# Recurrent attention into an ELU feed-forward layer: decay weights by summed logarithms on TensorE and ScalarE instead of scans on VectorE

## The chip, the cores and the metric

The kernel runs on one core of a Trainium2 chip. The metric is the device time of one execution in microseconds (us); smaller is better. The core has a matrix engine (TensorE, PE in the rows; its weight loads are PEld), a vector engine (VectorE, DVE), an activation engine (ScalarE, ACT), a general engine (GpSimd, POOL) and a queue engine (SyncE, SP) that issues all the DMA transfers here. Each engine runs its own instructions in program order and waits on semaphores for the others.

## What is computed

The reference is a recurrence over 768 steps for 4 batches of 8 heads of width 40, and then a feed-forward layer on all 3072 tokens (320 to 2048 to 320):

```python
for t in range(S):
    m_new = np.maximum(f_gate[:, :, t] + m, i_gate[:, :, t])
    f_stab = np.exp(f_gate[:, :, t] + m - m_new)
    i_stab = np.exp(i_gate[:, :, t] - m_new)
    m = m_new
    C = f_stab * C + i_stab * outer(vt, kt)
    n = f_stab * n + i_stab * kt
    y[:, :, t] = o * (C @ qt) / np.maximum(np.abs(n . qt), 1.0)
h = x @ w_in
g = np.where(h > 0.0, h, np.exp(np.minimum(h, 0.0)) - 1.0)
out = g @ w_out
```

## The kernel before

The recurrence is done in chunks of 128 steps. There are 6 chunks (`c`) and 4 batches (`b`), so 24 token blocks, n = 4c + b, called t0 to t23; each holds 128 tokens of all 8 heads. For one token block TensorE makes the products of keys and queries (`products`, L572), the weight of source step s at target step t is the product of the decays between them, the weighted products are multiplied with the values (`outputs`, L648; from chunk 1 on also the state of the earlier chunks, L640), and the state C of the batch is brought up to date (`update`, L661; the keys are first scaled by the last weights, `wl`). A result goes through a division, a gate and a transpose (L719) and is split in a high and a low part, `xh` and `xl`.

**The weights of a block.** For each half of the heads (4 heads, a tile of 128 x 512) VectorE runs a scan (`decays`, L612) along the targets: state = decay times state plus an identity entry. The decays must stand on all 128 partitions. For the first two chunks TensorE spreads them: `spread` (L598) multiplies a selecting matrix with the decays, cut in three bf16 parts (`parts`, L469 and L471), into a PSUM tile of the pool `h`, which has two buffers and serves the feed-forward layer's first results and the weight conversions too. From chunk 2 on a DMA does it. The input gates' factors are turned by TensorE (L484) and multiplied into the values (`va`, L580).

**The feed-forward layer** works on groups of two or three token blocks (2, 3, 3, ...) and 16 groups of 128 hidden units (f). One step is a first layer into `h` (eight matmuls, L772, 256 or 384 columns), an ELU on ScalarE and VectorE (L780, L783, L785), a split in two parts (L788, L790), and a second layer (L799). The first units of work are t0-t1 with f 0 to 7, t2-t4 with f 0 to 7, t5-t7 with f 0 to 7, and then t0-t1 again with f 8 to 15. The feed-forward weights come in as 64-bit words and are converted on the chip, 18 conversions c0, c1, ...; each is two ScalarE operations (L327, L332), three on VectorE (L336, L341, L346), one on GpSimd (L351), a rounding on ScalarE (L357) and the difference on VectorE (L361) or, for four of them, on TensorE (L369, L370).

**What sets the order.** All operations are recorded with the engines that may run them and a cost for each, and a list planner (`Plan.run`) then puts them out: by rank, then by the longest tail, on the engine that would end first, as far as the pools have room (`room`). `FIRST` gives the ranks of the first token blocks (t) and conversions (c). So an edit to costs, pools or operations moves instructions on every engine.

Of the kernel before, what the change touches and what calls it, by code (L numbers as in the profile page):

```python
# [11 lines left out]
F32 = mybir.dt.float32  # L12
# [8 lines left out]
P = 128  # L21
# [162 lines left out]
def tile_mlstm_then_elu_ffn(  # L184
# [27 lines left out]
    SPREAD_BY_PE = 2  # L212
# [6 lines left out]
    FIRST = "t0c0c4t1c5c6c1c2t2c8c3c7c9"  # L219
# [7 lines left out]
        wide=3, narrow=2, gates=2, rest=1, qk=3, bb=3, vko=3, w=3, va=2, wl=2, dec=2, den=2, xf=2,  # L227
# [27 lines left out]
    for name in room:  # L255
        if name not in ("ps_a", "h", "acc", "qk", "bb", "rest"):
            pool(name)
    pools["rest"] = ctx.enter_context(tc.tile_pool(name="rest", bufs=1))
# [127 lines left out]
    fgs = const.tile([3 * BH, SPREAD_BY_PE * L], BF16, name="fgs")  # L386
# [18 lines left out]
    def setup():  # L405
# [11 lines left out]
        op({"port": 1, "POOL": 0.8, "DVE": 0.4}, select, (("ident", 0),), (("sel", 0),))  # L417
        op({"POOL": 0.7, "DVE": 0.6},
# [12 lines left out]
    def gate_chunk(c):  # L431
# [18 lines left out]
        def log_decay(e):  # L450
            nc.vector.tensor_add(f(), f(), m()[:, 0:L])
            nc.vector.tensor_sub(f(), f(), m()[:, 1:])

        op({"port": 1, "DVE": 0.54}, log_decay, (KM,), (KF,))
        op({"port": 1, "POOL": 0.4, "DVE": 0.27}, lambda e: eng[e].tensor_sub(i(), i(), m()[:, 1:]), (KM,), (KI,))
        op({"ACT": 0.3}, lambda e: nc.scalar.activation(f(), f(), AF.Exp), (), (KF,))
# [7 lines left out]
        def parts(e):  # L464
            starts(e)
            rest = [f()] + [pools["rest"].tile([BH, L], F32, name=f"rest{j}") for j in range(2)]
            for j in range(3):
                part = fgs[j * BH : (j + 1) * BH, c * L : (c + 1) * L]
                nc.vector.tensor_copy(part, rest[j])  # L469
                if j < 2:  # L470
                    nc.vector.tensor_sub(rest[j + 1], rest[j], part)  # L471

        if c < SPREAD_BY_PE:
            op({"port": 1, "DVE": 1.5}, parts, (KF,), (FI, KF, ("fgs", c)))
        else:
            op({"port": 1, "DVE": 0.2}, starts, (KF,), (FI, KF))
            op({"SP": 0.06}, lambda e: nc.sync.dma_start(f_d[c], f()), (KF,), (("f_d", c),),
               nbytes=BH * L * 4)
# [9 lines left out]
        if c > 0:  # L488

            op({"port": 1, "DVE": 0.42},  # L490
# [39 lines left out]
    def attention(n):  # L530
# [15 lines left out]
        def va():  # L546
            return T("va", n, P, H, E)
# [381 lines left out]
```

## Time and profile before

| | |
|---|---|
| time of the three runs | 488.93, 490.2, 491.02 us; median 490.2 |
| span of the profiled execution, first to last instruction | 485.9 us |
| TensorE busy | 457.6 us, 94% of the span |
| VectorE busy | 366.3 us, 75% |
| ScalarE busy | 299.1 us, 62% |
| GpSimd busy | 85.5 us, 18% |

The profile gives no time of its own for the profiled execution beside its span; the median of the runs is 4.3 us over the span. The busy shares are means over a beginning, in which blocks are prepared and weights converted, and a long rest. Whether an engine is a limit is read by stretch. The granted clock of TensorE is one of two levels, 2.4 GHz (1.00) and 1.2 GHz (0.50).

### The profile page before, as it was taken

The page shows a single profiled execution, that of the slowest core. Times are in us where ns is not written, and L with a number is a line of the kernel's source. Part 1 is how long each engine was busy: PE and PEld are TensorE (multiplying, and loading weights), DVE is VectorE, ACT ScalarE, POOL GpSimd, SP SyncE. Part 2 cuts the span into 40 slices and gives each one's busy share as a digit, 9 for nine tenths or more (in the row PEclk, how much of TensorE's full clock was granted, in tenths as well). Part 3 has the DMA queues.
Part 4 walks back from the last instruction along what each step waited for, and adds up shares of the span by engine and source line. Part 5 has one row for each costly group of instructions (what it writes and reads, how often), then busy time and mean ns, then how long its engine had stood idle before and what let it go on. Part 6 is the DMA issues. An engine that isn't in the chain of part 4 may idle for free.

```text
span 485.9 us, 13150 instructions
## 1 busy us (share of the span) xinstructions
PE 457.6 (94%) x5342; PEld 429.9 (88%) x5342; DVE 366.3 (75%) x733; ACT 299.1 (62%) x753; POOL 85.5 (18%) x99
## 2 busy tenths in 40 slices
PE   2877889999999999999999999999999999999997
PEld 2554778899989999998999999999999999999996
DVE  8998799998988998959686578848778635446543
ACT  3778866668877555655456456665546654655764
POOL 3542263342230142212010002000001000000000
PEclk9779899999999999999999999999999999999999
DMA  7576454323325264424332233413324200100000
GB/s 254 184 222 210 137 167 138 112 99 125 109 82 155 77 191 138 136 72 125 102 109 69 76 89 107 125 40 113 112 89 137 70 1 1 42 1 4 28 0 28
DMA packets 39004, 49.56 MB, mean 102 GB/s; under 512 B 3072, under 2 KB 31648, under 8 KB 38944
## 3 DMA queue, kind: packets, MB, share of 16 engines
q1 hardware_dynamic: 38944, 48.72, 32.2%
q8 instruction: 42, 0.69, 0.6%
q14 instruction: 18, 0.15, 0.1%
HBM read 43.32 MB, written 5.39 MB: 100 GB/s over the span
## 4 chain that ended last, share of the span: by engine, by line
PE 80%; DVE 12%; ACT 3%; DMA 2%; issue 1%; SPq 1%; POOL 0%; DVEq 0%; ACTq 0%
PE h L772 35%; PE acc L799 32%; PE ps_a L572 5%; PE ps_a L648 2%; PE ps_a L640 2%; PE ps_a L719 1%; PE ps_a L661 1%; DMA qk<-in_qk 1%; DVE vko L698 1%; DVE C L672 1%; DVE w L612 1%; DVE e L785 1%; DVE gl L790 1%; DVE w L361 1%; ACT e L783 1%
## 5 line engine op out<-in xcount | busy, mean ns | idle before, releaser
L772 PE MATMUL h<-xh,w 128*128 128x384 f32 (+1 forms) x720 | 182.1, 326 | 3.8 <-DVE w L612 2.8
L799 PE MATMUL acc<-w,gh 128*128 128x320 f32 x768 | 173.6, 313 | 1.3 <-DVE w L361 1.2
L772 PEld LDWEIGHTS h<-xh,w 128*128 128x128 f32 x720 | 126.7, 190 | 7.1 <-DVE w L612 3.6
L799 PEld LDWEIGHTS acc<-w,gh 128*128 128x128 f32 x768 | 128.1, 188 | 3.3 <-DVE w L361 1.4
L799 PE MATMUL acc<-w,gl 128*128 128x320 f32 x384 | 119.2, 310 | 1.3 <-DVE gl L790 1.3
L785 DVE SCALAR_TENSOR_TENSOR e<-e,h 128x384 f32<-128x384 f32 (+1 forms) x144 | 72.8, 505 | 59.4 <-ACT e L783 58.6
L772 PE MATMUL h<-xl,w 128*128 128x384 f32 (+1 forms) x432 | 113.0, 320 | 2.0 <-DVE w L361 2.0
L780 ACT ACTIVATE e<-h 128x384 f32<-128x384 f32 (+1 forms) x144 | 65.4, 454 | 71.3 <-PE h L772 65.0
L790 DVE TENSOR_TENSOR gl<-e,gh 128x384 fp32r<-128x384 f32 (+1 forms) x126 | 68.7, 546 | 31.6 <-ACT gh L788 30.9
L788 ACT CAST gh<-e 128x384 fp32r<-128x384 f32 (+1 forms) x144 | 68.0, 472 | 31.1 <-DVE e L785 30.3
L772 PEld LDWEIGHTS h<-xl,w 128*128 128x128 f32 x432 | 77.7, 191 | 2.2 <-DVE w L361 2.2
L799 PEld LDWEIGHTS acc<-w,gl 128*128 128x128 f32 x384 | 72.2, 188 | 2.1 <-DVE gl L790 1.9
L783 ACT ACTIVATE e<-e 128x384 f32<-128x384 f32 (+1 forms) x144 | 70.5, 490 | 3.6
L612 DVE TENSOR_TENSOR_SCAN w<-w,ident 128x512 f32<-128x512 f32 x32 | 39.2, 1231 | 5.2 <-DMA w<-f_d 5.2
L351 POOL TENSOR_TENSOR narrow<-narrow,wide 128x512 int32<-128x512 int32 (+1 forms) x18 | 26.8, 1489 | 51.7 <-DVE narrow L346 20.2
L587 ACT ACTIVATE vko<-vko 128x320 f32<-128x320 f32 x72 | 33.4, 466 | 1.4 <-DMA vko<-in_vko 0.6
L626 DVE TENSOR_TENSOR w<-ps_a,w 128x512 f32<-128x512 f32 x48 | 31.4, 680 | 1.8 <-PE ps_a L572 1.8
L572 PE MATMUL ps_a<-qk 40*128 40x128 f32 x384 | 30.4, 298 | 0.0
L572 PEld LDWEIGHTS ps_a<-qk 40*128 40x128 f32 x384 | 25.6, 199 | 5.0 <-issue 3.5
L790 POOL TENSOR_TENSOR gl<-e,gh 128x384 fp32r<-128x384 f32 (+1 forms) x18 | 17.9, 994 | 58.2 <-ACT gh L788 49.3
L580 POOL TENSOR_TENSOR va<-vko,iT 128x320 f32<-128x320 f32 x16 | 12.8, 804 | 69.9 <-PE ps_a L661 28.2
L648 PE MATMUL ps_a<-va,w 128*32 128x41 f32 x1536 | 20.7, 207 | 3.5 <-DVE w L626 3.4
(96 smaller groups left out, 417.9 us busy)
## 6 DMA issues: line engine op xcount, KB each, us to landing
vko<-in_vko SPq DMA_DIRECT2D x24, 480.0 KB
w<-f_d SPq DMA_DIRECT2D x32, 256.0 KB
qk<-in_qk SPq DMA_DIRECT2D x48, 160.0 KB
wide<-in_w_out SPq DMA_DIRECT2D x8, 640.0 KB
wide<-in_w_in SPq DMA_DIRECT2D x8, 512.0 KB
out<-os SPq DMA_DIRECT2D x24, 160.0 KB
bb<-b_d SPq DMA_DIRECT2D x40, 80.0 KB
sum<-os SPq DMA_DIRECT2D x8, 160.0 KB
```

Source lines behind the costliest of these rows:

```text
L572: nc.tensor.matmul(ps(two, P, HH, L)[:, j, :], kt[rows, j, :], qt[rows, j, :], start=True, stop=True,)
L587: lambda e, fn=fn, kw=kw: nc.scalar.activation(v3()[2], v3()[2], fn, **kw), (), (KS,))
L612: nc.vector.tensor_tensor_scan(a, f, ident4.rearrange("p h t -> p (h t)"), 0.0, op0=ALU.mult, op1=ALU.add)
L626: lambda e, half=half: nc.vector.tensor_mul(w(half), ps(half, P, HH, L), w(half)),
L648: nc.tensor.matmul(y[r, h, :], w()[:, i, r], va()[:, h, :], start=not opened, stop=(i == H - 1), skip_group_check=True,)
L772: nc.tensor.matmul(h(), a[g][:, fs], m, start=(i == 0), stop=(i == len(prods) - 1))
L780: op(act(N), lambda e, h=h, ff=ff: nc.scalar.activation(ff("e"), h(), AF.Relu, scale=-1.0), (KHP,), (KE,))
L783: lambda e, ff=ff: nc.scalar.activation(ff("e"), ff("e"), AF.Exp, scale=-1.0), (), (KE,))
L785: lambda e, h=h, ff=ff: nc.vector.scalar_tensor_tensor(out=ff("e"), in0=ff("e"), scalar=-1.0, in1=h(), op0=ALU.add, op1=ALU.max),
L788: op(act(N), lambda e, ff=ff: nc.scalar.copy(ff("gh", F32R), ff("e")), (KE,), (KG,))
L790: lambda e, ff=ff: eng[e].tensor_sub(ff("gl", F32R), ff("e"), ff("gh", F32R).bitcast(F32)),
L799: nc.tensor.matmul(acc(a), x[:, sl], bw[g][:, j, :], start=(f == f0 and i == 0), stop=(f == f1 - 1 and i == 2),)
```

## The change

Five things change in the program.

First, for chunks 0 and 1 (`LOGS = 2`) the weights are no longer scanned. The logarithms of the decays are summed along the chunk on 32 partitions (one short scan), the input gate's logarithm minus that sum is put beside it, and both are cut in three bf16 parts (`lcs`, two rows of 128 instead of one). TensorE then makes the logarithm of every weight in an `h` tile from a mask (0, or minus 2 to the 100th where the source is later than the target), the source's term and the target's term, and one exponential on ScalarE writes the weights. The input gate is within them, so in these chunks no turned factor and no multiplication of the values is needed.

Second, the values come with a column of room for the ones from the DMA, and `va` is a view of that tile.

Third, the state update is part of `outputs`. It writes to the same PSUM tile as the outputs, in pieces of 32 and 8 columns, so `outputs` also waits for the scaled keys, and a token block takes one tile less of `ps_a`.

Fourth, `FIRST` is another list. Fifth, with the new operations the planner's order is another one on every engine.

```diff
-    SPREAD_BY_PE = 2
+    LOGS = 2
-    FIRST = "t0c0c4t1c5c6c1c2t2c8c3c7c9"
+    FIRST = "t0c3t1c4c0c1t2c2c5c6c9c10c11"
...
-        wide=3, narrow=2, gates=2, rest=1, qk=3, bb=3, vko=3, w=3, va=2, wl=2, dec=2, den=2, xf=2,
+        wide=3, narrow=2, gates=2, qk=3, bb=3, vko=3, w=3, wl=2, dec=2, den=2, xf=2,
...
+        if c < LOGS:
+            def sums_of_logs(e):
+                nc.vector.memset(lc()[:, 0, 0:1], 0.0)
+                nc.vector.tensor_tensor_scan(
+                    lc()[:, 0, 1:], f()[:, 1:], first[:, 1:], 0.0, op0=ALU.add, op1=ALU.min)
...
+            op({"port": 1, "DVE": 0.27}, lambda e: nc.vector.tensor_sub(lc()[:, 1], i(), lc()[:, 0]), (KI,), (KLC,))
...
+            def parts(e):
+                for j in range(3):
+                    part = lcs[j * BH : (j + 1) * BH, c]
+                    nc.vector.tensor_copy(part, lc())
+                    if j < 2:
+                        nc.vector.tensor_sub(lc(), lc(), part)
...
-                for j in range(HH):
-                    r = b * H + heads[half * HH + j]
+                mine = [b * H + h for h in heads[half * HH : (half + 1) * HH]]
+                nc.tensor.matmul(
+                    logs(), ident_b, mask.unsqueeze(1).to_broadcast([P, HH, L]),
+                    start=True, stop=False, skip_group_check=True,
+                )
+                nc.tensor.matmul(
+                    logs(), lcs[:, c, 1],
+                    sel[:, mine[0] : mine[-1] + 1 : 2].unsqueeze(2).to_broadcast([3 * BH, HH, L]),
+                    start=False, stop=False, skip_group_check=True,
+                )
+                for j, r in enumerate(mine):
                     nc.tensor.matmul(
-                        T("h", ("w", n, half), P, HH, L)[:, j, :],
-                        sel[:, r : r + 1].to_broadcast([3 * BH, P]),
-                        fgs[:, c * L : (c + 1) * L], start=True, stop=True,
+                        logs()[:, j, :], sel[:, r : r + 1].to_broadcast([3 * BH, P]), lcs[:, c, 0],
+                        start=False, stop=(j == HH - 1), skip_group_check=True,
                     )
...
-            if c < SPREAD_BY_PE:
-                op({"DVE": 1.23}, decays, (KP, ("ident4", 0)), (KW,))
+            if c < LOGS:
+                op({"PE": 0.8}, spread,
+                   (("sel", 0), ("lcs", c), ("mask", 0), ("ident_b", 0), ("w", n, "room")), (KP,))
+                op(act(HH * L),
+                   lambda e, half=half, logs=logs: nc.scalar.activation(w(half), logs(), AF.Exp), (KP,), (KW,))
...
+            if c < NC - 1:
+                for j in range(HH):
+                    for two, rows in enumerate(ROWS):
+                        for a, z in ((0, 32), (32, D)):
+                            nc.tensor.matmul(
+                                state()[rows.start + a : rows.start + z, j, :],
+                                v3()[1][:, 2 * j + two, a:z], va()[:, 2 * j + two, :],
+                                start=True, stop=True, skip_group_check=True,
+                            )
```

The order of the instructions moves with it. The first place is VectorE's work on the gates of chunk 0, up to what the first spread waits for. Before, the decays are cut in parts (`fgs`) and the first long scan follows:

```order
L452 TENSOR_TENSOR gatesf_158<-gatesf_158,gatesm_188 32x128
L455 TENSOR_TENSOR gatesi_166<-gatesi_166,gatesm_188 32x128
L461 COPY first_130<-gatesf_158 32x1
L462 MEMSET gatesf_158 32x1
L469 CAST fgs_131<-gatesf_158 32x128
L471 TENSOR_TENSOR rest0_204<-gatesf_158,fgs_131 32x128
L469 CAST fgs_131<-rest0_204 32x128
L471 TENSOR_TENSOR rest1_205<-rest0_204,fgs_131 32x128
L469 CAST fgs_131<-rest1_205 32x128
L580 TENSOR_TENSOR va_216<-vko_168,iT_133 128x8x40
L612 SCALAR_TENSOR_TENSOR w_229<-h_218,ident4_134 128x512
```

Now the logarithms are bounded (L467), summed (L480), subtracted (L484) and cut (L494 and L496, of which two more casts and one more difference follow):

```order
L465 TENSOR_TENSOR gatesf_154<-gatesf_154,gatesm_190 32x128
L467 TENSOR_SCALAR gatesf_154<-gatesf_154 32x128
L479 MEMSET gateslc_199 32x1
L480 SCALAR_TENSOR_TENSOR gateslc_199<-gatesf_154,first_124 32x127
L470 TENSOR_TENSOR gatesi_162<-gatesi_162,gatesm_190 32x128
L484 TENSOR_TENSOR gateslc_199<-gatesi_162,gateslc_199 32x128
L494 CAST lcs_125<-gateslc_199 32x256
L496 TENSOR_TENSOR gateslc_199<-gateslc_199,lcs_125 32x256
```

The chain to the first spread has more steps, and the steps of the cutting have twice the columns; the two exponentials that stood in it on ScalarE are gone.

The second place is TensorE at the end of block t0's weights. Before, a head's spread is one weight load and one matmul of 128 columns, and outputs and update follow as 32 and 8 instructions:

```order
L598 LDWEIGHTS sel_132
L598 MATMUL h_256<-fgs_131,sel_132 128x128
L648 MATMUL ps_a_269<-va_216,w_229 32x41 x32
L661 MATMUL ps_a_306<-va_216,vko_168 40x41 x8
L598 LDWEIGHTS sel_132
```

Now the half begins with two matmuls of 512 columns (mask and source term), and the update stands in pieces of 32 and 8 columns that alternate, 16 in all, in the outputs' own tile:

```order
L633 LDWEIGHTS ident_b_127
L633 MATMUL h_259<-mask_126,ident_b_127 128x512
L637 LDWEIGHTS lcs_125
L637 MATMUL h_259<-sel_128,lcs_125 128x512
L643 LDWEIGHTS sel_128
L643 MATMUL h_259<-lcs_125,sel_128 128x128
...
L695 MATMUL ps_a_272<-vko_164,w_243 32x41 x32
L705 MATMUL ps_a_272<-vko_164 32x41
L705 MATMUL ps_a_272<-vko_164 8x41
```

The third place is ScalarE after the fourth first-layer step of the feed-forward layer (`e` and `gh` are that layer's, `narrow` and `wide` a conversion's). Before, the layer goes on:

```order
L780 ACTIVATE e_801<-h_757 128x256
L732 CAST xl_669<-ps_a_788 128x3x128
L788 CAST gh_818<-e_793 128x256
L783 ACTIVATE e_801<-e_801 128x256
L357 CAST w20_123<-narrow_755 128x640
L235 COPY va_834<-iT_133 128x8
L327 ACTIVATE narrow_836<-wide_689 128x640
L332 ACTIVATE wide_689<-wide_689 128x640
L780 ACTIVATE e_851<-h_809 128x256
L788 CAST gh_860<-e_801 128x256
```

Now the same engine runs the exponentials of three chunk 1 blocks there, between pieces of conversions, and the layer's fifth step comes some 30 instructions later:

```order
L658 ACTIVATE w_855<-h_842 128x512
L837 CAST gh_864<-e_837 128x256
L358 CAST w21_118<-narrow_753 128x640
L333 ACTIVATE wide_702<-wide_702 128x512
L658 ACTIVATE w_855<-h_871 128x512
L658 ACTIVATE w_906<-h_884 128x512
L328 ACTIVATE narrow_916<-wide_702 128x512
L237 COPY wl_929<-w_906 128x4
L658 ACTIVATE w_906<-h_909 128x512
L620 ACTIVATE vko_637<-vko_637 128x320
```

What moved there: the conversions of the second group of first-layer weights (c5, c6) and the blocks t4 to t6 now stand after the fourth step of the feed-forward layer, where c5 and c6 stood ahead of the first step before.

## Rows read from the trace of the kernel before

**Rows 1.** Busy time of each engine by stretch, with granted clock and DMA.

```profile
core 0: us, PE busy (x) PEld busy (x) DVE busy (x) ACT busy (x) POOL busy (x), PEclk, DMA share, GB/s
0.00:12.00 12.00, 2.75 (x23) 2.55 (x25) 9.70 (x25) 4.10 (x12) 3.79 (x13) 1.00 0.76 253
12.00:24.00 12.00, 9.92 (x141) 6.67 (x143) 11.56 (x19) 8.45 (x22) 6.12 (x7) 0.79 0.56 180
24.00:36.00 12.00, 8.71 (x192) 6.41 (x185) 11.58 (x22) 8.72 (x24) 5.39 (x6) 0.78 0.75 227
36.00:48.00 12.00, 9.04 (x124) 6.23 (x122) 10.45 (x21) 10.46 (x25) 3.28 (x4) 0.93 0.63 209
48.00:60.00 12.00, 9.40 (x58) 8.23 (x59) 9.43 (x25) 9.57 (x25) 3.82 (x3) 0.78 0.48 150
60.00:72.00 12.00, 9.92 (x171) 8.86 (x169) 11.46 (x20) 8.71 (x24) 7.73 (x8) 1.00 0.54 165
72.00:84.00 12.00, 11.29 (x200) 10.56 (x201) 11.57 (x25) 7.20 (x22) 4.44 (x7) 1.00 0.43 141
...
144.00:192.00 48.00, 47.27 (x513) 45.67 (x513) 42.52 (x89) 28.27 (x80) 11.39 (x14) 1.00 0.46 136
```

**Rows 2.** Chain that ended last, from 36 to 86 us, by line.

```profile
by line: PE h L772 16.2%; DVE w L612 6.8%; DVE w L361 5.9%; PE ps_a L572 5.1%; DVE e L785 4.8%; DVE den L693 4.6%; SPq L526 4.2%; DVE w L626 3.9%; issue 3.9%; DMA gatesi<-in_i_gate 3.4%; DVE narrow L346 3.0%; DVE vko L698 3.0%; DMA b_d<-gat
```

**Rows 3.** TensorE's waits over the whole span: total, times, longest.

```profile
PE ps_a L484 <- ACT gatesi L457: 8.1, 1, 8.1
PE h L772 <- DVE w L612: 2.8, 3, 1.1
```

**Rows 4.** Groups of instructions by shape: count, busy us, mean ns, idle before.

```profile
L612 DVE TENSOR_TENSOR_SCAN w<-h,ident 128x512 f32<-128x512 f32 x16 | 19.0, 1206 | 0.4 <-PE h L598 0.4
...
L471 DVE TENSOR_TENSOR rest<-gatesf,fgs 32x128 f32<-32x128 f32 x2 | 0.6, 279 | 0.1
...
L341 DVE TENSOR_SCALAR narrow<-narrow 128x512 int32<-128x512 int32 x10 | 5.9, 590 | 0.2
...
L357 ACT CAST w<-narrow 128x512 fp32r<-128x512 f32 x8 | 4.9, 616 | 0.8 <-POOL narrow L351 0.8
...
L327 ACT ACTIVATE narrow<-wide 128x512 f32<-128x512 f32 x10 | 6.7, 670 | 2.2 <-DVE w L361 2.2
```

**Rows 5.** TensorE in order of time: start, length, line, operation, count.

```profile
9.53 1.01 PE L598 MATMUL h<-fgs,sel 96*128 96x128 bf16 x8 [1.17 <-DVE fgs L469]
...
42.52 0.38 PE L772 MATMUL h<-xh,w 128*128 128x256 f32 x1
...
73.89 0.78 PE L640 MATMUL ps_a<-C,bb 104*32 104x82 f32 x32
74.49 0.80 PE L648 MATMUL ps_a<-va,w 128*32 128x41 f32 x64
75.22 0.51 PE L661 MATMUL ps_a<-va,vko 128*40 128x41 f32 x16
75.66 0.56 PE L799 MATMUL acc<-w,gh 128*128 128x320 f32 x2
...
76.64 0.34 PE L772 MATMUL h<-xh,w 128*128 128x384 f32 x1
...
131.84 0.28 PE L772 MATMUL h<-xh,w 128*128 128x256 f32 x1
```

**Rows 6.** The chain around 113 us: start, length, work.

```profile
111.73 1.32 PE acc L799 x9
113.05 1.39 PE h L772 x8
114.44 1.09 PE ps_a L572 x16
```

**Rows 7.** Busy time in two of five short stretches at the low clock.

```profile
19.00:22.50 3.50, 3.50 (x20) 2.22 (x16) 3.50 (x5) 2.69 (x8) 2.29 (x2) 0.51 0.58 184
...
50.00:53.00 3.00, 3.00 (x18) 2.78 (x19) 2.96 (x6) 2.17 (x5) 0.10 (x1) 0.50 0.92 298
```

More of the change, by code (lines that the diff above doesn't have):

```diff
@@ L255, in tile_mlstm_then_elu_ffn @@
     for name in room:
-        if name not in ("ps_a", "h", "acc", "qk", "bb", "rest"):
+        if name not in ("ps_a", "h", "acc", "qk", "bb"):
             pool(name)
-    pools["rest"] = ctx.enter_context(tc.tile_pool(name="rest", bufs=1))
     pool("ps_a", PSUM)
@@ L384, in tile_mlstm_then_elu_ffn @@
     first = const.tile([BH, L], F32, name="first")
-    fgs = const.tile([3 * BH, SPREAD_BY_PE * L], BF16, name="fgs")
+    lcs = const.tile([3 * BH, LOGS, 2, L], BF16, name="lcs")
+    mask = const.tile([P, L], BF16, name="mask")
+    ident_b = const.tile([P, P], BF16, name="ident_b")
     sel = const.tile([3 * BH, BH], BF16, name="sel")
@@ L462, in starts @@
             nc.vector.memset(f()[:, 0:1], 0.0)
[L464 to L471, printed above, removed]
-        if c < SPREAD_BY_PE:
[L474 to L478, printed above, removed]
+        op({"port": 1, "DVE": 0.2}, starts, (KF,), (FI, KF))
+        op({"SP": 0.06}, lambda e: nc.sync.dma_start(f_d[c], f()), (KF,), (("f_d", c),),
+           nbytes=BH * L * 4)
         def turned():
@@ L542, in v3 @@
         def v3():
-            t3 = T("vko", n, P, 3, H, D)
-            return [t3[:, j] for j in range(3)]
+            rest = T("vko", n, P, H * E + 2 * H * D)[:, H * E :].rearrange("p (j h d) -> p j h d", j=2, d=D)
+            return [va()[:, :, 0:D], rest[:, 0], rest[:, 1]]
         def va():
-            return T("va", n, P, H, E)
+            return T("vko", n, P, H * E + 2 * H * D)[:, 0 : H * E].rearrange("p (h e) -> p h e", e=E)
         def w(half=None):
@@ L652, in outputs @@
                 opened = True
-        KY, KU = ("ps_a", (n, "y")), ("ps_a", (n, "u"))
-        op({"PE": 1.6 if c else 0.9}, outputs,
-           (("w", n, 0), ("w", n, 1), ("va", n, 0), ("va", n, 1)) + (KB + (("C", b),) if c else ()), (KY, ("given", n)))
-        if c < NC - 1:
-            def update(e):
-                for h in range(H):
-                    nc.tensor.matmul(
-                        ps("u", P, HH, E)[ROWS[h % 2], h // 2, :], v3()[1][:, h, :], va()[:, h, :],
-                        start=True, stop=True, skip_group_check=True,
-                    )
-            op({"PE": 0.5}, update, (KK, ("va", n, 0), ("va", n, 1), ("given", n)), (KU,))
+            if c < NC - 1:
[6 more added lines that the diff above has]
+                                start=True, stop=True, skip_group_check=True,
+                            )
+        KY = ("ps_a", (n, "y"))
+        op({"PE": (1.6 if c else 0.9) + (0.36 if c < NC - 1 else 0.0)}, outputs,
+           (("w", n, 0), ("w", n, 1), KV) + (KB + (("C", b),) if c else ())
+           + ((KK,) if c < NC - 1 else ()), (KY, ("given", n)))
+        if c < NC - 1:
             if c > 0:
@@ L908 @@
         ),
[L909 removed]
+        "vko": np.concatenate(
+            [
+                t(np.pad(x, ((0, 0), (0, 0), (0, 0), (0, p))), (0, 2, 1, 3)).reshape(4, 768, -1)
+                for x, p in ((v, 1), (k, 0), (o_gate, 0))
+            ],
+            axis=2,
+        ),
         "i_gate": np.ascontiguousarray(i_gate),
```

83 lines of the change are left out of this document (53 added, 30 removed).

## The prediction

> **What bounds the kernel now.** I read the busy time by stretch first [rows 1]. From 144 us on TensorE is busy 47.3 of 48 us: the rest of the kernel is TensorE's. The beginning is not. From 12 to 84 us TensorE is busy 58.3 of 72 us, so it idles 13.7 us, while VectorE is busy 66.1 of 72 us. The chain of waits says the same: from 36 to 86 us the scans, the weight differences, the ELU and the divisions on VectorE stand in it between the first-layer matmuls [rows 2]. TensorE's own waits name the scan too, 2.8 us in three waits ahead of first-layer matmuls, since a spread tile holds one of the two `h` buffers until the scan has read it [rows 3].
>
> In the beginning TensorE also loses time at the low clock. Five short stretches, 19 to 26, 33 to 36 and 46 to 53 us, show a granted clock of 0.50 to 0.54 [rows 7]; about 16 us of work ran there at half speed, so about 8 us are lost. The first work, from 9.5 to 15 us, is slow as well: eight spread matmuls take 1.01 us [rows 5], and outputs and update of a block, 1.2 us at speed, took about twice that; some 2.5 us more.
>
> I take three marks from the order of time [rows 5]: the first first-layer matmul at 42.5 us, the first one of 384 columns (second group of token blocks) at 76.6 us, and the first one of the fourth unit (t0-t1, second half of the hidden units) at 131.8 us, called M. Both orders have nine products, eight transposes, four conversions' differences and 24 first-layer steps ahead of M, so M can be compared; behind it both programs have the same work for TensorE and nearly no idle time. The forecast is made of how far M moves.
>
> **The change, part by part.** *Scans.* Sixteen scans of 1.206 us leave VectorE [rows 4], all ahead of M: minus 19.3 us.
>
> *Logarithms.* Per chunk five operations of 32x128 and two tiny ones go and four of 32x128 and five of 32x256 come. At 0.279 us [rows 4] for the old ones, and between that and twice that for the doubled width, a chunk costs 1.1 to 2.5 us more; I take 1.5, so plus 3 us for both. This also lies ahead of the first weights. The first spread now starts at 9.5 us [rows 5]; with 1.5 us more of chain, and one more memset ahead of it on VectorE, I put it at 11.3 us.
>
> *What the planner hands to VectorE.* By the orders of before and after, 24 small or middling operations come to VectorE ahead of M (copies of last weights and states, three scalings of keys, memsets, two ELU differences, two weight differences) and 7 go. Between 0.279 and 0.590 us each [rows 4] these 17 are 4.7 to 10 us; I take 7, for many are copies of a few columns. So VectorE's relief ahead of M is 19.3 - 3 - 7 = 9.3 us, half of what the scans cost.
>
> *Exponentials.* Sixteen come to ScalarE. No row has an exponential of 128x512 from PSUM; the cast of that shape takes 0.616 us, the absolute value 0.670 [rows 4]. Plus 10 us ahead of M, less about 2 for the turned factors' copies. ScalarE is busy 50 us of the first 72 [rows 1], so there is room, but not everywhere.
>
> *Spread on TensorE.* Per half two matmuls of 512 columns come. Eight of 384 take 1.39 us at full clock [rows 6], 0.174 each, so 512 columns take 0.23 us; at the low clock eight of 128 columns take 1.01 us [rows 5], so 512 take 0.5. Thirty-two are 7.4 to 16 us. Half of the blocks fall where the clock was low half of the time, so I take 9.5 us. The two turns of the factors go (0.5 us). It lies in the 13.7 us of idle time if VectorE leaves TensorE waiting anyhow; without that cover all of it is lost.
>
> *State update.* Twenty blocks with 16 matmuls in place of 8. The trace shows two records for each. The update now takes 0.44 us, from 75.22 to 75.66, for 16 records, 27.5 ns each; the outputs, of the same 32-column form that the new pieces have, take 0.73 us for 64 records, 11.4 ns each [rows 5]. So 32 records take 0.36 us at the outputs' rate and 0.88 at the present update's: from -1.5 to +8.8 us for twenty. The form is the outputs' own, so I go by their rate, and count 0 because pieces of 8 columns have no row. The Trainium skill speaks against this edit: "TensorE: Matmul & The Clock Gate", section "Wait — 56ns, not 53.3ns?", says that starts of matmuls never come closer than about 25 ns, however few columns they have. By that the update would be 0.80 us and twenty cost 7.2 us more; the outputs' 11.4 ns a record stands against the rule, as these rotate over four column positions.
>
> *Fused wait.* Outputs now wait for the scaled keys as well. Behind them on TensorE wait the next block's spread and the first layer. In the list the scaling starts with the last weights, as the product with the weights does, so it ends at about the same time; 0 to 0.5 us for each of eight blocks. A tile of `ps_a` less per block works the other way. I count 0 for both.
>
> **Sum by stages.** *To the first first-layer matmul.* VectorE was busy 43.3 of the first 48 us [rows 1], the end of which is this mark's first ELU. Eight scans go (-9.6 us); two conversions (c5, c6, three operations of about 0.6 us each) move behind it (-3.5); logarithms, copies and scalings come (+5.5). That is 7.6 us less, but the start is later by 1.8 us and the weights now pass through three engines. I put the mark at 38.5 us, 4 us earlier.
>
> *To the second mark.* Now 34.1 us. In it now come the two conversions, seven spreads in place of four and three blocks in place of two. TensorE's work there at full clock is 7.4 (first layer, 8 steps of 256 columns) + 5.3 (36 second-layer matmuls at 1.32 us for nine) + 3.3 (three products at 1.09 [rows 6]) + 5.3 (three blocks at 0.59 + 0.73 + 0.44 [rows 5]) + 5.6 (seven spreads at 0.8) + about 3.8 (transposes and differences) = 31 us. ScalarE was busy about 26 us of the 34 (its share of [rows 1]) and gets seven exponentials (4.3) and two conversions (5): 35 us. ScalarE and TensorE are both near the bound here, so I take 36 us: the mark falls at 74.5, 2 us earlier.
>
> *To M.* Now 55.2 us, almost all TensorE's. One block and one product less stand in it, two spreads less and three second-layer matmuls less: about 4 us. So 51 us, and M falls at 125.5 to 126, 6 us earlier.
>
> Behind M nothing changes by these numbers. So 485.9 - 5.8 = 480.1 us for the span, and with the 4.3 us by which the median of the runs is above it **484.4 us**. Counted on TensorE alone: its work to M rises by 9 us, so of 13.7 us of idle time and 10.5 us of lost clock about 15 must go. That is much, and is why I do not take more.
>
> **The rivals.**
>
> *All of VectorE's relief counts.* If the marks follow VectorE's 9.3 us, as [rows 2] would have it, M comes at 122.5 us and the time is 481; with a clock that stays high in the denser beginning 2 to 4 us better, 477 to 481. Against it: ScalarE and TensorE are then both full.
>
> *TensorE or ScalarE becomes the bound.* The spread's 9.5 us replace the idle time one for one, the later first spread adds its 1.8, and M stays at 129 to 134: 487.7 to 492.6, no change that can be told. For it speaks the sum on TensorE; against it that the idle time is where VectorE was full.
>
> *The update pays by the instruction.* At 27.5 ns a record it costs 8.8 us in twenty blocks, and the time goes to 493. The outputs' rows speak against it. By the floor that the Trainium skill states (the same page) it would go to about 492.
>
> *Slower: the spreads hold both `h` buffers.* The place is after the fourth first-layer step, where six spreads stand in a row on TensorE and their exponentials lie on ScalarE between conversions of 0.62 and 0.67 us [rows 4]. Each spread waits for the exponential two before it; if two such operations are ahead of each, a spread takes 2 us in place of 0.8. Seven in that stage and nine others make 16 x 1.2 = 19 us, of which the idle time hides about half: M at 137 to 140, 496. It decides when the second mark comes later than about 81 us. For it speaks that the same tile held TensorE up before [rows 3]; against it that an exponential is half as long as a scan.
>
> **How the numbers follow.** A change of 0.5% (2.4 us) is about what a measurement of this kernel can tell from none. Forecast, 481.5 to 487.7: 0.45. More relief, below 481.5: 0.20. New bound, 487.7 to 492.6: 0.17. Update by the instruction, about 492 to 493: 0.03, half on either side of the limit. Slower by the buffers, above 492.6: 0.15. So faster 0.65, same 0.19, slower 0.16. The range, 477.5 to 492.5, leaves out the best tenth and the slower rival.
>
> **What would show it.** No scan from PSUM, and sixteen exponentials of about 0.62 us. The first spread near 11.3 us; the three marks near 38.5, 74.5 and 126. TensorE idle from 12 us to M at 4 to 8 us instead of 14. Waits of first-layer or spread matmuls on the exponentials below 3 us in total; over 8 would be the slower rival. Outputs with update at 1.2 us or less for chunk 0 at full clock; 1.6 would be the update's present rate. Behind M, TensorE without idle time of more than 2 us. Wrong I would be most easily in the second stage, where I took 36 us between two full engines.

## The result and the profile after

The changed kernel takes **477.22 us** (median of four runs, 476.07 to 478.75), the kernel before, timed beside it, 489.56 us (487.69 to 491.02). The ratio is 0.9748 with a 95% interval of 0.9719 to 0.9776, so it is 12.3 us faster. The forecast was 484.4 us, and the result lies 0.3 us below the range.

The first view is the busy time of each engine by stretch, of the kernel after; the columns are those of [rows 1]. Behind the twelve-us stretches stand two stretches with a low clock, the three stages between the marks, all of 12 us to M, and two short stretches of the beginning.

```profile
core 0: us, PE busy (x) PEld busy (x) DVE busy (x) ACT busy (x) POOL busy (x), PEclk, DMA share, GB/s
12.00:24.00 12.00, 10.96 (x256) 7.15 (x254) 10.08 (x20) 10.47 (x23) 3.53 (x7) 1.00 0.61 204
24.00:36.00 12.00, 7.88 (x132) 5.46 (x133) 11.53 (x25) 10.09 (x27) 4.13 (x4) 0.72 0.79 232
36.00:48.00 12.00, 10.56 (x171) 8.65 (x167) 11.39 (x29) 10.46 (x26) 2.98 (x5) 1.00 0.65 203
48.00:60.00 12.00, 10.78 (x180) 8.20 (x184) 10.12 (x20) 9.27 (x22) 4.04 (x6) 0.86 0.51 159
60.00:72.00 12.00, 11.93 (x237) 9.67 (x222) 11.55 (x30) 10.64 (x30) 4.95 (x7) 1.00 0.79 230
72.00:84.00 12.00, 12.00 (x196) 11.79 (x196) 11.76 (x29) 11.18 (x27) 4.10 (x3) 1.00 0.48 146
...
144.00:192.00 48.00, 47.04 (x662) 44.79 (x662) 41.94 (x82) 26.92 (x75) 11.31 (x14) 1.00 0.46 135
...
29.00:36.00 7.00, 5.92 (x112) 3.97 (x114) 6.66 (x15) 5.62 (x16) 2.63 (x3) 0.52 0.92 273
...
49.50:53.50 4.00, 4.00 (x18) 2.87 (x18) 2.26 (x6) 3.21 (x8) 0.80 (x2) 0.57 0.85 249
...
0.00:40.12 40.12, 26.80 (x515) 17.90 (x515) 34.58 (x78) 27.60 (x64) 12.83 (x27) 0.91 0.70 217
40.12:74.55 34.43, 32.11 (x591) 26.54 (x591) 31.56 (x73) 29.25 (x75) 11.99 (x13) 0.95 0.63 190
74.55:123.36 48.81, 48.39 (x441) 46.88 (x440) 46.20 (x87) 42.70 (x93) 16.00 (x15) 1.00 0.40 126
12.00:123.36 111.36, 103.06 (x1522) 88.35 (x1521) 103.34 (x211) 96.07 (x222) 37.40 (x41) 0.95 0.54 167
...
8.00:12.00 4.00, 2.46 (x15) 1.46 (x14) 2.82 (x11) 1.11 (x3) 0.00 (x0) 1.00 1.02 313
12.00:15.80 3.80, 3.80 (x21) 2.04 (x20) 2.41 (x6) 2.92 (x5) 0.72 (x1) 1.00 0.80 314
```

And the same row, from 12 us to its own M, of the kernel before:

```profile
12.00:131.84 119.84, 105.67 (x1374) 91.84 (x1373) 109.23 (x201) 88.80 (x216) 47.36 (x47) 0.93 0.48 153
```

VectorE is still full from 24 to 48 us and again from 60 to 84, but TensorE has no idle time to speak of from 60 us on, where it was at 9.92 of 12 in [rows 1]. In the rows from 12 us to M I take TensorE's idle time as length less busy time, and what the low clock costs as length times (1 - granted clock), since at half speed one of two us is lost. Before: 14.2 us idle and 8.4 lost. After: 8.3 idle and 5.6 lost. These two fall by 8.7 us together, and M falls by 8.5. What is left of the stretch is 97.3 us before and 97.5 after. The clock is given to two decimals, so a loss is good to about 0.6 us.

TensorE in order of time, of the kernel after, with the places that answer to [rows 5]:

```profile
6.17 2.89 PE L602 MATMUL ps_a<-qk 40*128 40x128 f32 x16 [6.17 <-DMA qk<-in_qk]
8.99 0.61 PE L633 MATMUL h<-mask,ident_b 128*128 128x512 bf16 x1
11.13 0.61 PE L637 MATMUL h<-sel,lcs 96*128 96x512 bf16 x1 [1.53 <-DVE lcs L494]
...
13.24 0.63 PE L633 MATMUL h<-mask,ident_b 128*128 128x512 bf16 x1
13.66 0.63 PE L637 MATMUL h<-sel,lcs 96*128 96x512 bf16 x1
...
16.84 0.39 PE L633 MATMUL h<-mask,ident_b 128*128 128x512 bf16 x1
17.06 0.38 PE L637 MATMUL h<-sel,lcs 96*128 96x512 bf16 x1
...
17.60 1.16 PE L602 MATMUL ps_a<-qk 40*128 40x128 f32 x16
18.69 0.39 PE L633 MATMUL h<-mask,ident_b 128*128 128x512 bf16 x1
18.92 0.38 PE L637 MATMUL h<-sel,lcs 96*128 96x512 bf16 x1
...
22.16 0.81 PE L695 MATMUL ps_a<-vko,w 128*32 128x41 f32 x64
22.77 0.49 PE L705 MATMUL ps_a<-vko 128*32 128x41 f32 x32
23.20 0.39 PE L633 MATMUL h<-mask,ident_b 128*128 128x512 bf16 x1
...
40.12 0.28 PE L821 MATMUL h<-xh,w 128*128 128x256 f32 x1
...
74.55 0.42 PE L821 MATMUL h<-xh,w 128*128 128x384 f32 x1
...
123.36 0.28 PE L821 MATMUL h<-xh,w 128*128 128x256 f32 x1
```

The three marks are the last rows: 40.12, 74.55 and 123.36 us, against 42.5, 76.6 and 131.8 in [rows 5]. A spread of 512 columns starts 0.42 us ahead of its follower at 13.24 and 0.23 us ahead at 18.69. Outputs and update take 1.04 us, from 22.16 to 23.20.

TensorE's waits, the groups that replace the scans of [rows 4], and the chain from 36 to 86 us by line, with one of its pieces, all of the kernel after:

```profile
PE ps_a L602 <- DMA qk<-in_qk: 6.2, 1, 6.2
PE ps_a L768 <- DVE xf L751: 3.9, 2, 3.0
PE acc L848 <- DVE gl L839: 2.7, 2, 2.3
PE h L637 <- DVE lcs L494: 1.5, 1, 1.5
PE h L821 <- DVE e L834: 1.2, 2, 0.7
PE h L370 <- POOL vko L610: 1.1, 1, 1.1
PE ps_a L778 <- ACT xh L774: 1.0, 1, 1.0
```

```profile
L658 ACT ACTIVATE w<-h 128x512 f32<-128x512 f32 x16 | 9.4, 596 | 5.7 <-PE h L643 5.7
...
L494 DVE CAST lcs<-gateslc 32x256 bf16<-32x256 f32 x6 | 3.0, 492 | 0.2
L496 DVE TENSOR_TENSOR gateslc<-gateslc,lcs 32x256 f32<-32x256 f32 x4 | 1.6, 412 | 0.2
```

```profile
by line: PE acc L848 16.4%; PE h L821 15.4%; DMA wide<-in_w_out 11.4%; issue 10.8%; DVE w L667 9.9%; DVE narrow L347 5.5%; DVE w L362 4.4%; DVE lcs L494 4.1%; DVE vko L747 2.8%; DVE xf L751 2.2%; DVE bb L624 2.0%; DVE e L834 2.0%; DVE narro
...
30.31 5.70 DMA wide<-in_w_out
```

The first matmul waits for its data now, and no longer for the factors (8.1 us in [rows 3]). The wait on a scan of [rows 3] is gone, and no wait on an exponential (ACT w L658) has come in its place. ScalarE waits for the spreads (5.7 us), not the other way round. In the chain the scans of [rows 2] are gone as well. The 11.4% of the weight loads (`wide<-in_w_out`) is one load that ran from 30.31 to 36.01 us; it is counted whole, but lies almost wholly ahead of 36 us, in the stretch in which TensorE is idle most (7.88 us busy of 12 from 24 to 36).

### The profile page after: what moved, and what is told of

Same layout as the page of the kernel before. It is cut to its first block, busy times and chain, and to the rows that moved or that the text cites. A ratio compares the mean times of both kernels' runs of the same rounds, so it can differ in the third digit from the quotient of the medians.

```text
span 477.0 us, 13843 instructions
## 1 busy us (share of the span) xinstructions
PE 454.9 (95%) x5692; PEld 426.1 (89%) x5692; DVE 350.8 (74%) x725; ACT 300.9 (63%) x740; POOL 90.5 (19%) x113
## 4 chain that ended last, share of the span: by engine, by line
PE 71%; DVE 15%; DMA 6%; issue 3%; ACT 2%; POOL 1%; DVEq 0%; POOLq 0%; ACTq 0%; SPq 0%
PE h L821 31%; PE acc L848 30%; PE ps_a L602 3%; DMA vko<-in_vko 2%; PE ps_a L687 2%; PE ps_a L695 2%; DMA w<-f_d 2%; DVE w L667 2%; DMA wide<-in_w_out 1%; DVE e L834 1%; PE ps_a L768 1%; DMA f_d<-gatesf 1%; DVE w L650 1%; DVE gl L839 1%; DVE narrow L347 1%
## 5 line engine op out<-in xcount | busy, mean ns | idle before, releaser
L821 PE MATMUL h<-xh,w 128*128 128x384 f32 (+1 forms) x720 | 178.5, 322 | 1.3 <-DVE e L834 1.2
L821 PEld LDWEIGHTS h<-xh,w 128*128 128x128 f32 x720 | 124.8, 188 | 3.4 <-DVE e L834 2.0
L821 PE MATMUL h<-xl,w 128*128 128x384 f32 (+1 forms) x432 | 111.4, 317 | 0.0
L839 DVE TENSOR_TENSOR gl<-e,gh 128x384 fp32r<-128x384 f32 (+1 forms) x125 | 66.1, 530 | 35.5 <-ACT gh L837 33.7
L821 PEld LDWEIGHTS h<-xl,w 128*128 128x128 f32 x432 | 76.4, 188 | 0.0
L650 DVE TENSOR_TENSOR_SCAN w<-w,ident 128x512 f32<-128x512 f32 x32 | 38.5, 1217 | 6.9 <-DMA w<-f_d 6.9
L352 POOL TENSOR_TENSOR narrow<-narrow,wide 128x512 int32<-128x512 int32 (+1 forms) x18 | 26.9, 1492 | 43.9 <-DVE narrow L347 11.4
L695 PE MATMUL ps_a<-vko,w 128*32 128x41 f32 x1536 | 19.8, 204 | 0.0
L695 PEld LDWEIGHTS ps_a<-vko,w 128*32 128x32 f32 x1536 | 18.1, 111 | 1.5 <-issue 1.3
```

The source lines that it names most:

```text
L650: nc.vector.tensor_tensor_scan(a, a, ident4.rearrange("p h t -> p (h t)"), 0.0, op0=ALU.mult, op1=ALU.add)
L695: nc.tensor.matmul(y[r, h, :], w()[:, i, r], va()[:, h, :], start=not opened, stop=(i == H - 1), skip_group_check=True,)
L821: nc.tensor.matmul(h(), a[g][:, fs], m, start=(i == 0), stop=(i == len(prods) - 1))
L839: lambda e, ff=ff: eng[e].tensor_sub(ff("gl", F32R), ff("e"), ff("gh", F32R).bitcast(F32)),
```

## The experiments

All 18 runs in one table. "List" is the list of first ranks; "loss" is the low clock's, worked out as above. Marks, idle time and loss come from the one profiled execution, whose time can be off the median: in e17 it took 488.9 us against a median of 484.1, in e15 485.6 against 487.8, so the columns of these two are read with care. The kernel before was timed beside each group of runs, with medians from 489.37 to 490.5 us. The kernel after was timed in the first group alone, four times, and its interval overlaps those of e3, e7, e8, e10 and e13; a difference against it of about 3 us or less is not clear of noise.

| run | median us | ratio to before, 95% | marks us | idle, loss us |
|---|---|---|---|---|
| before | 489.56 | | 42.5 76.6 131.8 | 14.2, 8.4 |
| after | 477.22 | 0.972 to 0.978 | 40.1 74.6 123.4 | 8.3, 5.6 |
| e1 after, old list | 489.05 | 0.997 to 1.001 | 46.7 78.2 134.1 | 15.4, 8.5 |
| e2 after, scans' load back | 489.32 | 0.997 to 1.001 | 46.2 85.3 135.6 | 14.7, 12.4 |
| e3 after, exponentials twice | 479.75 | 0.976 to 0.982 | 41.3 76.8 125.6 | 9.5, 6.8 |
| e4 after, masks three times | 480.95 | 0.978 to 0.984 | 41.8 79.4 128.7 | 6.1, 4.7 |
| e5 before, new list | 499.96 | 1.019 to 1.023 | 43.3 90.5 143.6 | 18.0, 11.8 |
| e6 before, short scans | 487.9 | 0.994 to 0.998 | 42.5 75.4 130.1 | 12.7, 7.1 |
| e7 after, c5 c6 ahead | 476.39 | 0.971 to 0.976 | 46.9 69.6 123.8 | 9.7, 3.4 |
| e8 after, update in 40 columns | 478.25 | 0.973 to 0.978 | 39.9 74.7 123.7 | 7.7, 5.6 |
| e9 update apart, new list | 488.32 | 0.994 to 0.999 | 43.2 80.7 133.5 | 11.7, 8.5 |
| e10 after, list cut behind c6 | 476.81 | 0.970 to 0.978 | 40.1 74.6 122.0 | 7.5, 3.3 |
| e11 after, old head in new list | 480.58 | 0.978 to 0.985 | 42.4 78.5 127.9 | 10.3, 8.1 |
| e12 after, old list, c3 c7 first | 485.38 | 0.987 to 0.993 | 46.2 77.9 131.4 | 13.5, 8.4 |
| e13 after, one cost changed | 480.67 | 0.977 to 0.984 | 40.5 76.1 125.9 | 9.9, 4.6 |
| e14 update apart, list cut | 485.66 | 0.989 to 0.995 | 43.1 79.2 132.1 | 9.6, 8.4 |
| e15 update apart, c5 c6 ahead | 487.75 | 0.993 to 0.997 | 47.3 71.2 128.8 | 12.6, 4.7 |
| e16 before, list cut | 498.02 | 1.014 to 1.021 | 43.7 90.6 143.5 | 17.7, 11.8 |
| e17 update apart, outputs' tile | 484.14 | 0.987 to 0.993 | 41.0 80.7 132.5 | 12.2, 9.6 |
| e18 update fused, own tile | 482.06 | 0.983 to 0.988 | 39.8 75.0 127.2 | 12.1, 4.6 |

The spans behind M lie between 350.3 and 354.9 us in all of them, so the large differences arise ahead of M; small ones can arise behind it.

**e1: the list alone taken back.**

```diff
-    FIRST = "t0c3t1c4c0c1t2c2c5c6c9c10c11"
+    FIRST = "t0c0c4t1c5c6c1c2t2c8c3c7c9"
```

> The changed kernel with the list of ranks of before; everything else is the change's, and the planner orders anew. Theory V (VectorE's relief makes the gain, whatever the list): 478 to 481 us, at most a third of the gain of 12 us lost. Rival O (the new list makes the gain, since it puts two conversions behind the first feed-forward steps): 484 to 489 us.

It gives nothing against before: 489.05 us, and the first mark comes 4 us later than before. The logarithms and the fused update are in it, but VectorE's relief is not. Its row from 12 us to its M:

```profile
12.00:134.05 122.05, 106.67 (x1507) 91.69 (x1505) 108.87 (x226) 95.79 (x219) 35.18 (x32) 0.93 0.47 151
```

VectorE is busy 108.9 us there, as in the kernel before (109.2), and 103.3 in the kernel after. The planner has filled the place of the scans with other work, such as copies of last weights and differences of the layer's results. So with the old list taking the scans away gives nothing, but what relief that stays would be worth under that list is not shown by this run.

**e2: the load of the scans put back.** The order is that of the changed kernel; behind each product with the weights VectorE runs one scan that nobody reads.

```diff
             nc.vector.tensor_mul(w(half), ps(half, P, HH, L), w(half))
+            if c < LOGS:
+                i4 = ident4[:, 0:3].rearrange("p h t -> p (h t)")
+                nc.vector.tensor_tensor_scan(spare, i4, i4, 0.0, op0=ALU.mult, op1=ALU.add)
```

> The changed kernel, in the same order, with a scan of 128x384 that nobody reads on VectorE after each of the sixteen products with weights of the first two chunks: about 16 x 0.93 = 15 us of VectorE's time put back where the scans were. Theory V (the beginning is VectorE's): 486 to 492 us, 9 to 15 us come back. Rival O (order and merged tile make the gain, VectorE has room): 477 to 481 us.

489.32 us: the whole gain is gone. The row of its first stage, from the busy time by stretch:

```profile
0.00:46.18 46.18, 31.85 (x514) 21.22 (x515) 41.48 (x85) 27.66 (x64) 13.72 (x27) 0.78 0.62 197
```

VectorE is busy 41.5 us of 46.2 there, and TensorE's granted clock falls to 0.78 (0.91 after). VectorE's busy time from 12 us to M rises by 13.7 us (117.0 against 103.3), and the time by 12.1. So in this order, which was planned without the load, work put back on VectorE costs almost us for us. What it would cost if the planner laid it anew is not shown.

**e3 and e4: more work for ScalarE and for TensorE**, in the same order: a second exponential of 128x512 behind each, unread; and the mask's matmul three times.

```diff
             nc.scalar.activation(w(half), logs(), AF.Exp)
+            nc.scalar.activation(spare, ident4.rearrange("p h t -> p (h t)"), AF.Exp)
```

> The changed kernel, in the same order, with a second exponential of 128x512, of data that nobody reads, after each of the sixteen: 16 x 0.62 = 10 us more on ScalarE. If ScalarE had become the bound of the second stage, as my step from the first to the second mark had it: 483 to 487 us. If VectorE is still the bound and ScalarE has room: 478 to 481 us.

```diff
-                nc.tensor.matmul(
-                    logs(), ident_b, mask.unsqueeze(1).to_broadcast([P, HH, L]),
-                    start=True, stop=False, skip_group_check=True,
-                )
+                for again in range(3):
+                    nc.tensor.matmul(
+                        logs(), ident_b, mask.unsqueeze(1).to_broadcast([P, HH, L]),
+                        start=again == 0, stop=False, skip_group_check=True,
+                    )
```

> The changed kernel, in the same order, with the mask's matmul of 512 columns three times in place of once in each half (the same weights: the sum is as far below zero): 32 matmuls more, 0.22 us each at full clock, 7 us, up to 10 with those at the low clock. If TensorE's idle time of the beginning covers them: 478 to 480 us. If TensorE is the bound already: 484 to 487 us.

From 12 us to M ScalarE is busy 6.8 us longer in e3 (102.8 against 96.1), and the time rises by 2.5; TensorE is busy 7.5 us longer in e4 (110.6 against 103.1), and the time rises by 3.7. ScalarE has room: e3's rise is not clear of noise. Of TensorE's extra work the idle time ahead of M takes 2.2 us (8.3 to 6.1), and M comes 5.3 us later in the profiled execution; TensorE has little room left there. The rival by which ScalarE or TensorE would be the new bound falls for ScalarE.

**e5 and e6: one part alone, in the kernel before.** e5 has only the new list. e6 keeps the old order and puts a copy in place of each of the 16 scans from PSUM, so it leaves out the product of the decays.

```diff
-    FIRST = "t0c0c4t1c5c6c1c2t2c8c3c7c9"
+    FIRST = "t0c3t1c4c0c1t2c2c5c6c9c10c11"
```

> The kernel before with the changed kernel's list of ranks and nothing else; the planner orders anew. Theory P (the list pays only where VectorE has been relieved, each alone gives nothing): 486 to 493 us. Rival O (the list alone is most of the gain): 478 to 482 us.

```diff
+                if c < SPREAD_BY_PE:
+                    nc.vector.tensor_copy(a, f)
+                    return
                 nc.vector.tensor_tensor_scan(
```

> The kernel before, in the same order, with a copy of the spread decays on VectorE in place of each of the sixteen scans from PSUM (what is left out: the product of the decays, so the weights are others): about 16 x 0.6 = 10 us less on VectorE, nothing else changed. Theory V (VectorE's time bounds the beginning in any order): 480 to 484 us. Rival P (relief pays only with the new list): 486 to 489 us.

e5 is 10.4 us slower than before (499.96). Its second stage, and TensorE's waits within it:

```profile
43.31:90.47 47.16, 35.81 (x406) 29.71 (x405) 38.59 (x75) 27.91 (x75) 16.29 (x18) 0.75 0.43 140
```

```profile
PE ps_a L572 <- DVE xf L702: 4.1, 1, 4.1
PE h L369 <- DVE w L612: 3.7, 1, 3.7
PE h L772 <- DVE w L361: 2.1, 1, 2.1
...
PE h L598 <- DVE w L612: 0.5, 2, 0.3
```

The stage that takes more blocks in the new order takes 47.2 us in place of 34.1; TensorE idles 11 us there, at a granted clock of 0.75. The scans hold the `h` tiles for 4.2 us of that. The longest wait, 4.1 us, is a product's for a tile of `ps_a` that VectorE (L702) has yet to read. e6 gains 2 us, though VectorE's busy time from 12 us to M falls by 6.3 (102.9 against 109.2). So the list alone loses and the relief alone gains 2 us, in an order that was planned with the scans; together, and with the fused update, they gain 12. The fused update alone, in the kernel before, was not run.

**e7, e10, e11 and e12: which part of the list.** In this order:

```diff
+    FIRST = "t0c3t1c4c0c5c6c1t2c2c9c10c11"
+    FIRST = "t0c3t1c4c0c1t2c2c5c6"
+    FIRST = "t0c0c4t1c3c1t2c2c5c6c9c10c11"
+    FIRST = "t0c0c4t1c5c6c1c2t2c3c7c8c9"
```

> The changed kernel with the conversions c5 and c6 put ahead of c1 in its list, where the old list had them. Theory: what the list gives is that the first feed-forward steps need not wait for these two conversions: 483 to 488 us. Rival (it is the rest of the list: c3 and c4 first, c9 to c11 early): 477 to 480 us.

> The changed kernel with the new list cut behind c6 (no c9, c10, c11), so that the third group of first-layer weights has only the planner's own rank. Theory 1, the new list gains by its head (c3 and c4 ahead of c0): first mark 40 as changed, time 475 to 479. Theory 2, it gains by its tail (the weights that the second group of hidden units needs come early): first mark 40, second mark or M later by 4 to 10 us, time 482 to 489.

> The changed kernel with the new list, but with the head's conversions as in the old one: c0 and c4 ahead of t1, c3 behind it. Theory 1 (the head gains): the first mark goes from 40 to 44 or later and the time to 483 to 489. Theory 2 (the tail gains): 475 to 479.

> The changed kernel with the old list, in which only c3 and c7 are put ahead of c8 (what the first steps need first comes first). If the old list loses since c8 takes the buffers and VectorE ahead of c3, which the very first step needs: 479 to 484 us and a first mark of 42 to 44. If the loss lies in the early c0 and c4: 486 to 490, first mark 46 to 47.

Where c5 and c6 stand moves the first mark from 40.1 to 46.9 and the second from 74.6 to 69.6, and leaves the time as it was, so the theory that stood ahead of e7 fails. The tail does nothing. The old head (c0, c4 ahead of c3) costs 3.4 us, and putting c3 and c7 ahead of c8 in the old list gets 3.7 of 11.8 back. Both are about what e13 below moves by the order alone, so where in the list its gain lies is not shown.

**e8: the update in 8 matmuls of 40 columns** in place of 16 of 32 and 8, still within the outputs.

```diff
-                        for a, z in ((0, 32), (32, D)):
+                        for a, z in ((0, D),):
```

> The changed kernel, in the same order, with the state update in 8 matmuls of 40 columns a block in place of 16 of 32 and 8, still in the outputs' tile. By the outputs' rate (no price by the instruction): 476.5 to 478 us, the same. By a price for each instruction: 470 to 474 us, since twenty blocks issue half as many.

478.25 us, no difference: in this kernel half as many instructions save nothing.

**e9, e14 and e15: the update as an operation of its own again**, with its own tile of `ps_a` and its own wait, under three lists that are good for the fused one (the new one, the cut one, the one with c5 and c6 ahead).

```diff
+            def update(e):
+                for h in range(H):
+                    nc.tensor.matmul(
+                        ps("u", P, HH, E)[ROWS[h % 2], h // 2, :], v3()[1][:, h, :], va()[:, h, :],
+                        start=True, stop=True, skip_group_check=True,
+                    )
+
+            op({"PE": 0.5}, update, (KK, KV, ("given", n)), (KU,))
```

> The changed kernel with the state update as an operation of its own again (8 matmuls of 40 columns, own PSUM tile, own wait); everything else as changed, list included; the planner orders anew. If the fused update has no part in the gain: 474 to 480 us. If the tile of ps_a that fusing frees, or the one wait less, carries part of it: 482 to 487 us, with more waits of the products on ps_a between 40 and 75 us.

> The update as an operation of its own, with the new list cut behind c6. The kernel with the fused update gave 476.8 us with this list, the separate update 488.3 with the whole new list. If the fused update is what is needed: 485 to 490. If the separate update only fell on a bad order: 475 to 481 with this other order.

> The update as an operation of its own, with c5 and c6 ahead of c1 in the new list. The fused one gave 476.4 us with this list. If the fused update is needed: 485 to 490. If only the order: 475 to 481 in this one or in the one with the cut list.

Each is far slower than the fused one under the same list: 11.1, 8.9 and 11.4 us. e9's row of TensorE up to M:

```profile
12.00:133.49 121.49, 109.81 (x1395) 93.05 (x1394) 108.26 (x220) 96.44 (x215) 40.69 (x38) 0.93 0.49 155
```

Of the 10.1 us by which its M is later, 3.4 are more idle time and 2.9 more loss; some 3 to 4 are not explained by these two. Two more things differ. The planner counts the separate update with 0.50 us, the fused one with 0.36; e13 below makes that change alone. And VectorE is busy 108.2 to 108.5 us from 12 us to M in the three runs, 5 us more than in the kernel after.

**e13: the order alone.** One number of the planner is altered, and nothing else.

```diff
-        op({"PE": (1.6 if c else 0.9) + (0.36 if c < NC - 1 else 0.0)}, outputs,
+        op({"PE": (1.6 if c else 0.9) + (0.5 if c < NC - 1 else 0.0)}, outputs,
```

> The changed kernel with one of the planner's numbers altered, the cost on TensorE by which it counts the update within the outputs, 0.50 in place of 0.36 us. Every instruction, tile and wait is as in the changed kernel; only the planned order differs (the first place is the fourth product, which comes behind a conversion's difference). If the gain belongs to the parts of the change: 475 to 480 us. If it belongs to the one order in which they were planned, and the separate update lost by another order alone: 483 to 489 us.

480.67 us, 3.5 slower with the same instructions (2.7 by the ratios to before, and the intervals touch). That is the size of what an order can do that nobody meant; differences of this size between the runs above are not laid on a part of the change. It is also the fairer base for e9, whose update has the same cost: against e13 the separate update loses 7.7 us, not 11.1.

**e16: the kernel before with the cut list.**

```diff
-    FIRST = "t0c0c4t1c5c6c1c2t2c8c3c7c9"
+    FIRST = "t0c3t1c4c0c1t2c2c5c6"
```

> The kernel before, scans and separate update and all, with the new list cut behind c6, on which the changed kernel does as well as with the whole one. If the logarithms are needed for any gain: 488 to 500 us. If the kernel before only lacked a good order: below 484.

498.02 us, as bad as e5, with the second mark at the same place (90.6).

**e17 and e18: the tile or the operation.** e17 keeps the update apart but writes it to the outputs' tile; e18 fuses it but writes it to a second tile.

```diff
-        KY, KU = ("ps_a", (n, "y")), ("ps_a", (n, "u"))
+        KY, KU = ("ps_a", (n, "y")), ("ps_a", (n, "y"), "u")
-                        ps("u", P, HH, E)[ROWS[h % 2], h // 2, :], v3()[1][:, h, :], va()[:, h, :],
+                        state()[ROWS[h % 2], h // 2, :], v3()[1][:, h, :], va()[:, h, :],
```

> The update as an operation of its own (own wait, 8 matmuls of 40 columns, counted 0.50 us), but written to the outputs' own tile, as in the changed kernel; so a block takes no more of ps_a than there. Theory tile: the fused update gained since a block asks for one PSUM tile less, 474 to 481 us here. Theory operation: it gained since the planner places one operation in place of two, 484 to 490 us here.

```diff
-                                state()[rows.start + a : rows.start + z, j, :],
+                                ps("u", P, HH, E)[rows.start + a : rows.start + z, j, :],
```

> The update within the outputs, one operation and one wait as in the changed kernel, but written to a second tile of ps_a, so that a block asks for two tiles at once. Theory tile: 484 to 492 us. Theory operation: 474 to 481 us.

Both lie between: 6.9 us lost with one tile but two operations, 4.8 with one operation but two tiles. e17 has the planner's cost of e13 as well, and loses 3.5 us against that run. Neither theory holds alone, and with e13's 3.5 us as the measure the split is not settled. VectorE's extra 5 us are not in these two (103.4 and 104.4 us busy from 12 us to M). That both together are worth 9 to 11 us is shown under three lists, with the changed cost in it; without that, under the new list, it is about 8.

## Why the prediction was wrong

**Right.** The direction, and the place: of the 8.9 us between the two profiled spans 8.5 lie ahead of M. The second mark was forecast at 74.5 and came at 74.55, by luck: the stage ahead of it was 1.6 us longer than forecast, its own 1.6 us shorter. The first spread came at 11.13 us (11.3 forecast). The logarithms cost about what was taken: the six casts and four differences are 4.6 us, where those of half the width were 2.5, and bound, sum and difference (L467, L480, L484) add 1.8. The exponential takes 0.596 us (forecast from rows of 0.616 and 0.670), no wait on it appears, and outputs with update take 1.04 us (at most 1.2 forecast). The slower rival, spreads that hold both `h` buffers, is not there.

**The update.** The counted price of 0 by the instruction held: 32 records from 22.77 to 23.20 us are 13 ns each, and e8 shows no difference. By the floor of about 25 ns that the Trainium skill states ("TensorE: Matmul & The Clock Gate", section "Wait — 56ns, not 53.3ns?") these 32 would take an estimated 0.80 us; the trace has 0.43 us and disagrees for this form.

**Wrong: "Fused wait ... I count 0 for both".** This is the step that failed most. I weighed the longer wait against the tile of `ps_a` and set both to nothing. e9, e14 and e15 show that the kernel after is 9 to 11 us slower with the update apart, and about 8 where the planner's cost is the same (e9 against e13). What differs is one operation, one tile and the order that the planner makes of them; how that becomes time is open (e17 and e18: neither alone accounts for it). I had looked for its price in TensorE's instructions, where there is none.

**Wrong: relief as a sum.** I counted VectorE's relief, 9.3 us, and let part of it through; the rival had all of it count. Both take it as a sum that holds in whatever order. VectorE's busy time from 12 us to M fell by 5.9 us only. With the old list it does not fall at all (108.9 us in e1, 109.2 before). Where the order is held, 6.3 us less on VectorE are worth 2 us in the old order (e6), and 13.7 us more cost 12 in the new one (e2). The list, which I had counted as a move of two conversions, is worth 12 us with the logarithms and the fused update (e1) and costs 10 without them (e5). The old list loses idle time and clock on TensorE with the logarithms as without: 15.4 and 8.5 us in e1, 14.2 and 8.4 before.

**Wrong: TensorE's work rises by 9 us.** From that I had judged a larger gain unlikely. TensorE's busy time from 12 us to M fell from 105.7 to 103.1 us, and what is left of the stretch beside idle time and loss is the same within the error of the loss. The spreads' 32 matmuls were sized about right: they start 0.22 us apart where the clock is high, so some 7 us, and e4's 32 more raise the busy time by 7.5. The sum left out what falls: nine second-layer matmuls (174 records in place of 183) now lie behind M, and the first layer's 192 are busy 33.4 us in place of 37.0, with less of the low clock.

**The sizes.** First stage 40.1 us (38.5 forecast), second 34.4 (36), third 48.8 (51). The third was forecast 4 us shorter than before and is 6.4 us shorter: TensorE's busy time in it fell from 54.05 to 48.39 us, and it is busy 48.4 of 48.8 us. The last mark is 2.7 us earlier than forecast, and behind M it is 0.4 us shorter. TensorE is idle 6.0 of 353.6 us there (4.9 of 354.1 before), where at most 2 had been forecast.

**The size of the gain.** The step that the number rests on is "485.9 - 5.8": M was to move by 5.8 us. In the profiled executions M moved by 8.5 and the span fell by 8.9 (485.9 to 477.0); from median to median the time fell by 12.3. The other 3.4 us come from which executions were profiled. That of the kernel after, 478.75 us, is the highest of its four. That of the kernel before has no time on record, but spans lie some 2 us under their times, so its 485.9 us belong to about 488, the low end of its four. Adding the 4.3 us was not the error: 480.1 + 4.3 is the old median less 5.8. Of the miss of 7.2 us, 6.5 are the gain, and 0.6 is the median of before, 489.56 in place of 490.2.

That M came within 3 us of its forecast was then partly luck: the fusing was counted at nothing, and without it the gain is 2.2 to 4.5 us (e9, e14, e15), less than the 5.8 forecast.

What stays open: how the fused update's 8 to 11 us divide between the tile and the operation, which of the list's places carry its gain, what the fused update would do in the kernel before, and the 3 to 4 us of e9 that neither idle time nor clock explains.

## What to carry to other kernels

Where a planner sets the order, an edit's worth is not the sum of its durations: here logarithms, list and fused update are worth 12 us together, nothing under the old list, 2 to 4.5 with the update apart in its own tile, and the list alone loses 10. Look, too, whether the relief is still there once the planner has placed the work anew: under the old list VectorE was as busy as before. Before a gain or loss is laid on an edit, change the order alone once (one cost, one rank) and see how far that moves the time; here it is about 3 us. And do not take one profile's gain for the gain: here two profiled executions are 8.9 us apart, the medians 12.3.

## What the hardware showed

The granted clock of the profile does not show the slow beginning. The rows of 8 to 12 and 12 to 15.8 us of the kernel after say 1.00, but 512 columns take 0.42 us there (13.24 to 13.66) and 0.22 us from 16.84 on (16.84 to 17.06), so the early spreads ran at about half the later speed. TensorE's first matmuls, a block's 16 products, took 2.8 us from 6.17 on, where the same 16 take 1.1 us from 17.60 on, and TensorE was idle for 1.5 us ahead of 11.13. This loss is in no column of the table above.
